# Routed attention and a feed-forward block in one kernel: scores, masks and values in quarters of the TensorE array, with centroid products, weight rounding and sums moved

## The chip, the cores and the metric

One Trainium2 chip; the kernel runs on one of its cores. The metric is the device time of one execution in microseconds (us). Engines are named as in the profile: PE is TensorE's matrix multiplication and PEld its loading of stationary weights, DVE is VectorE, ACT is ScalarE, POOL is GpSimd, SP is SyncE, which here issues nearly all DMAs. SBUF is the working memory, PSUM the accumulators that PE writes (eight banks of 512 float32 columns on 128 partitions), HBM the main memory.

## The reference

Inputs q, k, v are (4, 8, 768, 64) and centroids (8, 16, 64) in float32; the two weight matrices, (512, 2048) and (2048, 512), are in float64.

```python
def _attn_ref(q, k, v, centroids):
    q_n, k_n, c_n = (t / (norm(t) + 1e-06) for t in (q, k, centroids))
    q_assign = argmax(einsum('bhsd,hcd->bhsc', q_n, c_n))
    k_assign = argmax(einsum('bhsd,hcd->bhsc', k_n, c_n))
    mask = q_assign[:, :, :, None] == k_assign[:, :, None, :]
    scores = D ** -0.5 * matmul(q, k.transpose(0, 1, 3, 2))
    scores = where(mask, scores, -1e9)
    attn = softmax(scores)                    # with 1e-09 added to the sum
    return matmul(attn, v)

x = attn_out.transpose(0, 2, 1, 3).reshape(3072, 512)
h = x @ w_in
out = (h / (1 + exp(-1.702 * h))) @ w_out
```

Every query and every key is assigned to the nearest of its head's 16 centroids, and a query sees only keys of its own cluster. The attention's output goes through a feed-forward block with a sigmoid gate.

## The kernel before, in words

**Tiling of the attention.** There are 32 heads (4 batches of 8), taken two at a time: 16 pairs `p`, the two heads of a pair `a` = 0 and 1. The 64 dimensions of head 0 lie on partitions 0 to 63, those of head 1 on 64 to 127. A pair has two groups `g`, one for each half of the queries (384 of them, `HALF`); a group has six units `u`, one for each block of 128 keys (`kt`). For a unit the kernel computes transposed scores, 128 keys on the partitions and 384 queries along the row, for both heads (`scores`, L451); adds a mask term by a second product into the same PSUM tile (`part`, L466); takes the exponential on ACT into an SBUF tile `A` (`exps`, L474); adds `A` up over the six key blocks on POOL (`add_up`, L484, five additions per group); and multiplies by the values on PE, accumulating the group's output in PSUM (`values`, L495), which ACT then copies to SBUF (L501).

**Masks.** From the centroid products (`prep_near`, L326; sixteen small products per pair, into PSUM) DVE finds each row's best centroid and turns its number into a code (`prep_assign`, L349 to L389: a transposition, a maximum, a comparison, a product with ranks, a maximum, a square, a transposition, a cast). SP writes the codes to DRAM as lines (L396, four DMAs) and loads them back as rows (`prep_spread`, L403, sixteen DMAs of one row each). The mask product takes three such rows of keys and three of queries; it comes to zero where the codes agree and to a very large negative number where they do not. For the first pair the mask comes from one-hot vectors instead (`prep_hot`).

**Normalisation.** When a group's six units are through, PE sums `sum` over the keys (`normalise`, L508), DVE transposes, takes the reciprocal, spreads it back (L511, L513, L516) and multiplies the output by it (L522).

**Rounding of weights.** In the same phase DVE reads the 32 chunks of float64 weights as integers and makes float32 of them: five operations per chunk (`rounding`, L189, L193, L196, L200, L203), one at a time between other work (`step`). A chunk keeps one PSUM bank from its first operation to its last. ACT looks at each chunk for values out of range (`check_w`).

**Feed-forward block.** Both products use a seven-product scheme for 2 by 2 blocks (`first7`, `second7`), which needs sums and differences of weights (POOL) and of x (`sums_x`, DVE, L554).

**Order.** Every engine works through its instructions in the order in which the program issues them (`manual_schedule`). The main loop `for t in range(NT + 2)` makes one *step* of two units per pass; a pair is six steps, numbered here 0 to 5. In each pass: scores and masks of the step's two units, exponentials, POOL's additions; preparations of the next pair as `prep_at` has them (Q transposed on DVE, L305, in step 0; K transposed and centroid products in step 2; assignment and spread in step 3); values of the step before; some rounding operations, as many as `steps = (3, 1, 2, 0, 1, 4)` says; and, in steps 1 and 4, the row sums and the normalisation of the group that ended two steps before. Centroid products stand ahead of the values on PE. All eight sums of x for the first batch are issued together (`t == NT - 20`).

**PSUM.** `ps_m` has three banks, shared by rounding, centroid products, assignment and row sums; `ps_s` two tiles of two banks for scores; `ps_o` one bank for the values' sum. In the feed-forward block `ps_b` has five.

Of the kernel before, what the change touches and what calls it, by code (L numbers as in the profile page):

```python
# [8 lines left out]
FP32 = mybir.dt.float32  # L9
# [29 lines left out]
def fast(  # L39
# [26 lines left out]
    nc = tc.nc  # L66
# [155 lines left out]
    def check_w(i, raw, z):  # L222
# [123 lines left out]
    def prep_assign(p):  # L346
        ps = bank()
        if p > 0:
            nc.vector.transpose(out=ps[:, 0:HALF], in_=sT.pop(p)[:, 0:HALF])  # L349
# [41 lines left out]
    def prep_spread(p):  # L391
        n = NJ * 4
        row = code.pop(p)
        line = dram.tile([2, n, P], BF16, name="line")
        for r in range(0, P, SQ):
            nc.sync.dma_start(  # L396
                out=line[:, :, r:r + SQ].rearrange("b n t -> n b t"),
                in_=row[r:r + n])
        for a in range(2):
            for r in range(SQ * a, P, 2 * SQ):  # L400
                for w, b, to in ((0, 0, 0), (0, 1, 1), (1, 0, 0), (1, 1, 2)):
                    at = (w * 2 + a) * NJ
                    nc.sync.dma_start(  # L403
                        out=rows_of[w, p % 2][r + to:r + to + 1, :],
                        in_=line[b, at:at + NJ, :].rearrange(
                            "j t -> (j t)")[None, :])

# [37 lines left out]
    def scores(u):  # L445
        g, kt = divmod(u, NJ)
        p, h = split(g)
        ps = ps_s.tile([P, 2, 512], FP32, name="s")
        for a in range(2):
            rows = slice(a * D, (a + 1) * D)  # L450
            nc.tensor.matmul(out=ps[:, a, 0:HALF],  # L451
                             lhsT=T[p, 1][rows, kt * P:(kt + 1) * P],
                             rhs=T[p, 0][rows, h * HALF:(h + 1) * HALF],
                             start=True, stop=False)
        s_of[u] = ps[:, :, 0:HALF]

    def part(u):

        g, kt = divmod(u, NJ)
        p, h = split(g)  # L460
        n = NC if p == 0 else 3
        q_rows, k_rows = (hots[w] if p == 0 else rows_of[w, p % 2]
                          for w in range(2))
        for a in range(2):
            r = SQ * (a if p == 0 else 2 * (u % 2) + a)
            nc.tensor.matmul(  # L466
                out=s_of[u][:, a, :],
                lhsT=k_rows[r:r + n, kt * P:(kt + 1) * P],
                rhs=q_rows[r:r + n, h * HALF:(h + 1) * HALF],
                start=False, stop=True)  # L470

# [16 lines left out]
    def values(u):  # L488
        g, kt = divmod(u, NJ)
        p, h = split(g)  # L490
        if kt == 0:
            o_of[g] = ps_o.tile([P, 512], FP32, name="o")
        A = A_of.pop(u)
        for a in range(2):
            nc.tensor.matmul(out=o_of[g][a * D:(a + 1) * D, 0:HALF],  # L495
                             lhsT=v_in[p][:, a, kt, :], rhs=A[:, a, :],
                             start=(kt == 0), stop=(kt == NJ - 1))
        if kt == NJ - 1:
            O_of[g] = (xp if p < NPAIR - HP else xl).tile(
                [P, HALF], FP32, name="x")  # L500
            nc.scalar.copy(O_of[g], o_of.pop(g)[:, 0:HALF])  # L501

    def normalise(g):

        sm = sum_of.pop(g)
        ps = bank()
        for a in range(2):
            nc.tensor.matmul(out=ps[a * D:(a + 1) * D, 0:HALF], lhsT=twos,  # L508
                             rhs=sm[:, a, :], start=True, stop=True)
        turned = short()  # L510
# [9 lines left out]
        b, hp = divmod(p, HP)  # L520
        x = O_of.pop(g)
        nc.vector.tensor_tensor(out=x, in0=x, in1=rec, op=ALU.mult)  # L522
# [35 lines left out]

    def differences(b):


        X = {(r, h, c): xT_of.pop((b, h, 2 * r + c))
             for r in range(2) for h in range(2) for c in range(2)}
        T = {(3, c): T_of[3, c] for c in range(2)}
        for c in range(2):
            T[1, c] = X[0, 1, c]
            sums(nc.vector, ((T[3, c], X[1, 1, c], "-", T[1, c]),
                             (T[1, c], T[1, c], "-", X[0, 0, c])))
        return X, T

    def A_in(row, col, f):
# [23 lines left out]
    def sums_x(b):  # L598

        X, T = differences(b)  # L600
        T.update(((i, c), T_of[i, c]) for i in (2, 4) for c in range(2))
        for c in range(2):
            sums(nc.vector, ((T[2, c], X[1, 1, c], "-", T[1, c]),))
        for c in range(2):
            sums(nc.vector, ((T[4, c], X[1, 0, c], "-", T[2, c]),))
        return X, T

# [28 lines left out]
    for t in range(NT + 2):  # L636
# [167 lines left out]
    for b in range(B):  # L804
# [11 lines left out]
        for n in range(NH):  # L816
# [19 lines left out]
            if n == 1 and b < B - 1:  # L836
                XT = sums_x(b + 1)
    return is_bad
# [438 lines left out]
```

## Time and profile before

| | us |
|---|---|
| median of 3 runs | 996.82 (993.31 to 1000.97) |
| profiled execution | 997.54 |
| its span | 995.7 |
| first scores to the first product of the feed-forward block | 12.1 to 409.3 |
| feed-forward block | 409.3 to 995.7 |

| busy, us | span | PE | DVE | ACT | POOL |
|---|---|---|---|---|---|
| all | 995.7 | 943.0 | 623.8 | 314.3 | 418.8 |
| 46.0 to 368.0 | 322.0 | 288.8 | 257.0 | 184.2 | 252.6 |
| 409.3 to 995.7 | 586.4 | 581.0 | 320.8 | 88.8 | 105.0 |

A line of a group reads: source line, engine, operation, out<-in with shapes, count, then busy time, mean length of one, idle time of the engine just before them and what ended it. A line of the timeline reads: start, length, engine, line, operation, out<-in, count, and in brackets the idle time ahead of it and what ended it. A line of the waits reads: who waited, for whom, us in total, times, the longest. PE's float32 products appear as two matmul records each, so eight records of scores are the four products of a step. A record's length is that of the product passing through the array; the distance between starts says how long PE was taken.

### The profile page before, as it was taken

To read this page: it belongs to the slowest core of one execution; us is meant where nothing else is said; L and a number is where in the kernel's file an instruction comes from. 1 tells how busy PE (TensorE), PEld (TensorE's weight loads), DVE (VectorE), ACT (ScalarE), POOL (GpSimd) and SP (SyncE) were. 2 spreads that over 40 slices of the span, in tenths; PEclk is the share of its full clock that TensorE was granted. 3 is DMA by queue.
4 is the path that set the end of the run, shared out by engine and by line. 5 is a ranking of instruction groups with operands and counts; after the bars stand their busy time and mean duration, and the time that the engine had idled before them with its cause. 6 is when DMAs were issued, how large, how long until landed. Compare 5 with 4: busy or idle time off the path is not lost.

```text
span 995.7 us, 12731 instructions
## 1 busy us (share of the span) xinstructions
PE 943.0 (95%) x4565; PEld 569.6 (57%) x4565; DVE 623.8 (63%) x1029; ACT 314.3 (32%) x671; POOL 418.8 (42%) x308
## 2 busy tenths in 40 slices
PE   5998999999998789999999999999999999999997
PEld 3333333333333233455788655888655888556886
DVE  3678778877779985477634477534577434677431
ACT  3565565555655456322100122100222000222000
POOL 3878788777879678677400122000122000220000
PEclk8999999999999899999999999999999999999999
DMA  9344444544444311000200000000000000000000
GB/s 179 82 94 111 94 98 95 112 101 92 93 114 92 87 49 29 17 0 1 64 22 22 21 1 1 0 22 22 22 0 1 16 22 22 6 1 1 22 22 24
DMA packets 138440, 46.59 MB, mean 47 GB/s; under 512 B 127376, under 2 KB 132736, under 8 KB 138368
## 3 DMA queue, kind: packets, MB, share of 16 engines
q1 hardware_dynamic: 138224, 45.66, 20.2%
q8 instruction: 38, 0.62, 0.3%
q14 instruction: 34, 0.28, 0.1%
q10 hardware_dynamic: 144, 0.03, 0.0%
HBM read 37.63 MB, written 8.05 MB: 46 GB/s over the span
## 4 chain that ended last, share of the span: by engine, by line
PE 82%; DVE 12%; issue 3%; SPq 1%; DMA 1%; ACT 1%; POOL 0%; DVEq 0%; POOLq 0%; ACTq 0%
PE b L716 29%; PE b L773 29%; PE o L495 10%; PE s L451 9%; DVE T L305 2%; PE s L466 2%; PE m L508 2%; DVE short L516 1%; DVE short L511 1%; DVE e L200 1%; DVE x L522 1%; PE m L326 1%; DVE T L554 1%; DVE e L196 1%; DVE m L189 1%
## 5 line engine op out<-in xcount | busy, mean ns | idle before, releaser
L484 POOL TENSOR_TENSOR sum<-sum,A 128x768 f32<-128x768 f32 x128 | 243.3, 1901 | 32.0 <-ACT A L474 23.5
L474 ACT ACTIVATE A<-s 128x768 f32<-128x768 f32 x192 | 144.9, 806 | 158.6 <-PE s L466 157.0
L554 POOL TENSOR_TENSOR W<-w_in 128x256 f32<-128x256 f32 x32 | 23.8, 742 | 381.3 <-PE b L716 381.2
L707 DVE TENSOR_TENSOR G<-b,G 128x384 f32<-128x384 f32 x224 | 124.4, 556 | 64.6 <-PE b L716 51.4
L451 PE MATMUL s<-T,T 64*128 64x384 f32 x768 | 153.1, 518 | 4.4 <-ACT A L474 4.4
L495 PE MATMUL o<-A,inv 128*64 128x384 f32 x768 | 150.4, 515 | 0.0
L707 DVE TENSOR_TENSOR y<-b,y 128x256 f32<-128x256 f32 x72 | 29.4, 423 | 171.1 <-PE b L773 121.9
L544 ACT ACTIVATE th<-G 128x384 f32<-128x384 f32 x128 | 67.0, 523 | 210.1 <-DVE G L707 129.4
L451 PEld LDWEIGHTS s<-T,T 64*128 64x128 f32 x768 | 67.0, 189 | 89.6 <-ACT A L474 55.8
L545 DVE SCALAR_TENSOR_TENSOR G<-th,G 128x384 f32<-128x384 f32 x128 | 91.5, 715 | 22.8 <-ACT th L544 19.1
L716 PE MATMUL b<-x,W 128*128 128x384 f32 x256 | 93.0, 486 | 0.0
L716 PE MATMUL b<-T,w_in 128*128 128x384 f32 x256 | 93.0, 486 | 0.0
L716 PE MATMUL b<-x,w_in 128*128 128x384 f32 x256 | 89.9, 492 | 0.0
L773 PE MATMUL b<-Z,G 128*128 128x256 f32 x384 | 86.8, 379 | 0.0
L484 POOL TENSOR_TENSOR sum<-A 128x768 f32<-128x768 f32 x32 | 59.6, 1862 | 61.4 <-ACT A L474 61.3
L773 PE MATMUL b<-w_out,G 128*128 128x256 f32 x384 | 84.8, 379 | 0.0
L495 PEld LDWEIGHTS o<-A,inv 128*64 128x64 f32 x768 | 48.0, 140 | 57.0 <-issue 55.8
L773 PEld LDWEIGHTS b<-w_out,G 128*128 128x128 f32 x384 | 72.8, 190 | 10.9
L773 PEld LDWEIGHTS b<-Z,G 128*128 128x128 f32 x384 | 73.0, 190 | 9.9
L716 PEld LDWEIGHTS b<-x,w_in 128*128 128x128 f32 x256 | 49.1, 192 | 34.0 <-issue 1.2
L716 PEld LDWEIGHTS b<-x,W 128*128 128x128 f32 x256 | 48.6, 190 | 33.9
L716 PEld LDWEIGHTS b<-T,w_in 128*128 128x128 f32 x256 | 48.6, 190 | 33.9
(112 smaller groups left out, 1053.3 us busy)
## 6 DMA issues: line engine op xcount, KB each, us to landing
raw<-in_moe_w_in_dram SPq DMA_DIRECT2D x16, 512.0 KB
raw<-in_moe_w_out_dram SPq DMA_DIRECT2D x16, 512.0 KB
inv<-in_v_dram SPq DMA_DIRECT2D x16, 384.0 KB
in<-in_q_dram SPq DMA_DIRECT2D x60, 96.0 KB
in<-in_k_dram SPq DMA_DIRECT2D x60, 96.0 KB
rows<-line SPq DMA_DIRECT2D x240, 1.5 KB
out_dram<-y SPq DMA_DIRECT2D x12, 256.0 KB
out_dram<-y SPq DMA_DIRECT2D x24, 128.0 KB
```

The costliest lines, as they stand in the source:

```text
L305: nc.vector.transpose(out=T[p, w], in_=qk_in[p, w].rearrange("p j a d -> p (j a d)"))
L451: nc.tensor.matmul(out=ps[:, a, 0:HALF], lhsT=T[p, 1][rows, kt * P:(kt + 1) * P], rhs=T[p, 0][rows, h * HALF:(h + 1) * HALF], start=True, ...
L466: nc.tensor.matmul(out=s_of[u][:, a, :], lhsT=k_rows[r:r + n, kt * P:(kt + 1) * P], rhs=q_rows[r:r + n, h * HALF:(h + 1) * HALF], start=Fa ...
L474: nc.scalar.activation(out=A_of[u], in_=s_of.pop(u), func=AF.Exp, scale=SCALE)
L484: nc.gpsimd.tensor_tensor(out=sum_of[g], in0=A_of[u - 1] if kt == 1 else sum_of[g], in1=A_of[u], op=ALU.add)
L495: nc.tensor.matmul(out=o_of[g][a * D:(a + 1) * D, 0:HALF], lhsT=v_in[p][:, a, kt, :], rhs=A[:, a, :], start=(kt == 0), stop=(kt == NJ - 1))
L544: nc.scalar.activation(out=t, in_=h, func=AF.Tanh, scale=1.702)
L545: nc.vector.scalar_tensor_tensor(out=g, in0=t, scalar=1.0, in1=h, op0=ALU.add, op1=ALU.mult)
L554: engine.tensor_tensor(out=o, in0=a, in1=b, op=(ALU.add if op == "+" else ALU.subtract))
L707: nc.vector.tensor_tensor(out=o, in0=p, in1=a, op=ALU.add)
L716: nc.tensor.matmul(out=ps[:, 0:HALF], lhsT=a[:, c], rhs=x(c), start=(c == 0), stop=(c == 1))
L773: nc.tensor.matmul(out=ps[:, 0:DN], lhsT=a(f // 4)[:, f % 4], rhs=z(f), start=(f == 0), stop=(f == FB - 1))
```

## The change

- `scores`: each product of 64 dimensions by 128 keys becomes two of 64 by 64, so that a unit has four, one for each quarter of the array (64 rows by 64 columns).
- `part`: the mask rows of a head are laid out in a tile of 64 rows that is zero elsewhere, and the mask products are of 64 rows by 64 columns, four per unit instead of two. `rows_of` is set to zero and two single rows of each tile to `-CODE` (eight more memsets on POOL at the start). `prep_spread` loads eight rows per pair instead of sixteen.
- `values`: the 128 keys of a block are split into two halves of 64, accumulated in two banks (`ps_o` has two banks). ACT copies both halves, the second into a `short` tile, and `normalise` adds them on DVE before it multiplies.
- `normalise` is split: `row_sums_of` holds the products and stands directly behind the values.
- Centroid products come behind the values and row sums of step 2; K is transposed in step 1.
- `prep_assign` transposes into a `short` tile in SBUF, so that its maximum and its comparison read SBUF instead of PSUM (all pairs but the first). `tmp` has five tiles.
- Rounding: `steps = (2, 0, 4, 0, 1, 4)`. `ps_m` has two banks, `ps_b` six.
- `sums_x` is a generator that makes one sum at a time; those of the first batch are spread over the last eight steps.

```diff
-    ps_m = ctx.enter_context(tc.tile_pool(name="ps_m", bufs=3, space=PS))
+    ps_m = ctx.enter_context(tc.tile_pool(name="ps_m", bufs=2, space=PS))
...
-    tmp = att.enter_context(tc.tile_pool(name="tmp", bufs=3))
+    tmp = att.enter_context(tc.tile_pool(name="tmp", bufs=5))
...
-    for rows in rows_of.values():
-        nc.gpsimd.memset(rows, -CODE)
+    for (w, _), rows in rows_of.items():
+        nc.gpsimd.memset(rows, 0.0)
+        for r in range(SQ * w, P, D):
+            nc.gpsimd.memset(rows[r:r + 1, :], -CODE)
...
     def prep_assign(p):
-        ps = bank()
         if p > 0:
-            nc.vector.transpose(out=ps[:, 0:HALF], in_=sT.pop(p)[:, 0:HALF])
+            ps = short()
+            nc.vector.transpose(out=ps, in_=sT.pop(p)[:, 0:HALF])
         else:
+            ps = bank()
...
-            for r in range(SQ * a, P, 2 * SQ):
-                for w, b, to in ((0, 0, 0), (0, 1, 1), (1, 0, 0), (1, 1, 2)):
-                    at = (w * 2 + a) * NJ
-                    nc.sync.dma_start(
-                        out=rows_of[w, p % 2][r + to:r + to + 1, :],
+            for w, b, to in ((0, 0, 1), (0, 1, SQ), (1, 0, 1), (1, 1, 0)):
+                at, r = (w * 2 + a) * NJ, a * D + to
+                nc.sync.dma_start(
+                    out=rows_of[w, p % 2][r:r + 1, :],
...
     def scores(u):
...
-            nc.tensor.matmul(out=ps[:, a, 0:HALF],
-                             lhsT=T[p, 1][rows, kt * P:(kt + 1) * P],
-                             rhs=T[p, 0][rows, h * HALF:(h + 1) * HALF],
-                             start=True, stop=False)
+            for c in range(0, P, D):
+                nc.tensor.matmul(
+                    out=ps[c:c + D, a, 0:HALF],
+                    lhsT=T[p, 1][rows, kt * P + c:kt * P + c + D],
+                    rhs=T[p, 0][rows, h * HALF:(h + 1) * HALF],
+                    start=True, stop=False)
...
     def part(u):
...
         for a in range(2):
-            r = SQ * (a if p == 0 else 2 * (u % 2) + a)
-            nc.tensor.matmul(
-                out=s_of[u][:, a, :],
-                lhsT=k_rows[r:r + n, kt * P:(kt + 1) * P],
-                rhs=q_rows[r:r + n, h * HALF:(h + 1) * HALF],
-                start=False, stop=True)
+            rows = slice(a * D, (a + 1) * D)
+            for c in range(0, P, D):
+                nc.tensor.matmul(
+                    out=s_of[u][c:c + D, a, :],
+                    lhsT=rows_of[1, p % 2][rows, kt * P + c:kt * P + c + D],
+                    rhs=rows_of[0, p % 2][rows, h * HALF:(h + 1) * HALF],
+                    start=False, stop=True)
...
     def values(u):
...
-            o_of[g] = ps_o.tile([P, 512], FP32, name="o")
+            o_of[g] = ps_o.tile([P, 2, 512], FP32, name="o")
         A = A_of.pop(u)
-        for a in range(2):
-            nc.tensor.matmul(out=o_of[g][a * D:(a + 1) * D, 0:HALF],
-                             lhsT=v_in[p][:, a, kt, :], rhs=A[:, a, :],
-                             start=(kt == 0), stop=(kt == NJ - 1))
+        for r in range(2):
+            rows = slice(r * D, (r + 1) * D)
+            for a in range(2):
+                nc.tensor.matmul(out=o_of[g][a * D:(a + 1) * D, r, 0:HALF],
+                                 lhsT=v_in[p][rows, a, kt, :],
+                                 rhs=A[rows, a, :],
+                                 start=(kt == 0), stop=(kt == NJ - 1))
...
-            nc.scalar.copy(O_of[g], o_of.pop(g)[:, 0:HALF])
...
+                [P, HALF], FP32, name="x"), short()
+            for r in range(2):
+                nc.scalar.copy(O_of[g][r], o[:, r, 0:HALF])
...
-        x = O_of.pop(g)
+        x, more = O_of.pop(g)
+        nc.vector.tensor_tensor(out=x, in0=x, in1=more, op=ALU.add)
         nc.vector.tensor_tensor(out=x, in0=x, in1=rec, op=ALU.mult)
...
-            t = 2 * TG * (p - 1) + (0, 0, 2, 2, 2, 3, 3)[i]
+            t = 2 * TG * (p - 1) + (0, 0, 1, 1, 2, 3, 3)[i]
...
-    steps = (3, 1, 2, 0, 1, 4)
-    XT = None
+    steps = (2, 0, 4, 0, 1, 4)
+    made = sums_x(0)
...
-        while work and PREP[work[0][1]] == prep_near:
-            prep(*work.pop(0))
         if 1 <= t <= NT:
             for u in range(2 * t - 2, 2 * t):
                 values(u)
+        if t >= 2 and (t - 2) % TG == TG - 1:
+            row_sums_of((t - 2) // TG)
+        while work and PREP[work[0][1]] == prep_near:
+            prep(*work.pop(0))
...
-        if t == NT - 20:
-            XT = sums_x(0)
+        if t >= NT - 8 and t < NT:
+            XT = next(made)
...
-    ps_b = ctx.enter_context(tc.tile_pool(name="ps_b", bufs=5, space=PS))
+    ps_b = ctx.enter_context(tc.tile_pool(name="ps_b", bufs=6, space=PS))
```

More of the change, by code (lines that the diff above doesn't have):

```diff
@@ L399, in prep_spread @@
         for a in range(2):
[L400 to L406 removed]
+            for w, b, to in ((0, 0, 1), (0, 1, SQ), (1, 0, 1), (1, 1, 0)):
+                at, r = (w * 2 + a) * NJ, a * D + to
+                nc.sync.dma_start(
+                    out=rows_of[w, p % 2][r:r + 1, :],
+                    in_=line[b, at:at + NJ, :].rearrange(
+                        "j t -> (j t)")[None, :])
     def prep_hot(p):
@@ L460, in part @@
         p, h = split(g)
-        n = NC if p == 0 else 3
-        q_rows, k_rows = (hots[w] if p == 0 else rows_of[w, p % 2]
-                          for w in range(2))
-        for a in range(2):
-            r = SQ * (a if p == 0 else 2 * (u % 2) + a)
-            nc.tensor.matmul(
-                out=s_of[u][:, a, :],
-                lhsT=k_rows[r:r + n, kt * P:(kt + 1) * P],
-                rhs=q_rows[r:r + n, h * HALF:(h + 1) * HALF],
-                start=False, stop=True)
+        if p == 0:
+            for a in range(2):
+                r = SQ * a
+                nc.tensor.matmul(
+                    out=s_of[u][:, a, :],
+                    lhsT=hots[1][r:r + NC, kt * P:(kt + 1) * P],
+                    rhs=hots[0][r:r + NC, h * HALF:(h + 1) * HALF],
+                    start=False, stop=True)
+            return
+        for a in range(2):
+            rows = slice(a * D, (a + 1) * D)
+            for c in range(0, P, D):
+                nc.tensor.matmul(
+                    out=s_of[u][c:c + D, a, :],
+                    lhsT=rows_of[1, p % 2][rows, kt * P + c:kt * P + c + D],
+                    rhs=rows_of[0, p % 2][rows, h * HALF:(h + 1) * HALF],
+                    start=False, stop=True)
     def exps(u):
@@ L491, in values, with row_sums_of @@
         if kt == 0:
-            o_of[g] = ps_o.tile([P, 512], FP32, name="o")
+            o_of[g] = ps_o.tile([P, 2, 512], FP32, name="o")
         A = A_of.pop(u)
-        for a in range(2):
-            nc.tensor.matmul(out=o_of[g][a * D:(a + 1) * D, 0:HALF],
-                             lhsT=v_in[p][:, a, kt, :], rhs=A[:, a, :],
-                             start=(kt == 0), stop=(kt == NJ - 1))
+        for r in range(2):
+            rows = slice(r * D, (r + 1) * D)
+            for a in range(2):
+                nc.tensor.matmul(out=o_of[g][a * D:(a + 1) * D, r, 0:HALF],
+                                 lhsT=v_in[p][rows, a, kt, :],
+                                 rhs=A[rows, a, :],
+                                 start=(kt == 0), stop=(kt == NJ - 1))
         if kt == NJ - 1:
+            o = o_of.pop(g)
             O_of[g] = (xp if p < NPAIR - HP else xl).tile(
-                [P, HALF], FP32, name="x")
-            nc.scalar.copy(O_of[g], o_of.pop(g)[:, 0:HALF])
-    def normalise(g):
+                [P, HALF], FP32, name="x"), short()
+            for r in range(2):
+                nc.scalar.copy(O_of[g][r], o[:, r, 0:HALF])
+    def row_sums_of(g):
         sm = sum_of.pop(g)
-        ps = bank()
+        ps = ps_of[g] = bank()
         for a in range(2):
@@ L509, in normalise @@
                              rhs=sm[:, a, :], start=True, stop=True)
+    ps_of = {}
+    def normalise(g):
+        ps = ps_of.pop(g)
         turned = short()
@@ L557, in fast @@
     T_of = {}
[L559 to L569, printed above, removed]
     def A_in(row, col, f):
@@ L598, in sums_x @@
     def sums_x(b):
-        X, T = differences(b)
-        T.update(((i, c), T_of[i, c]) for i in (2, 4) for c in range(2))
+        X = {(r, h, c): xT_of.pop((b, h, 2 * r + c))
+             for r in range(2) for h in range(2) for c in range(2)}
+        T = {(i, c): T_of[i, c] for i in (2, 3, 4) for c in range(2)}
         for c in range(2):
[L603 to L606, printed above, removed]
+            T[1, c] = X[0, 1, c]
+        for o, a, z in ((3, (1, 1), 1), (1, 1, (0, 0)), (2, (1, 1), 1),
+                        (4, (1, 0), 2)):
+            for c in range(2):
+                one, two = (X[(*n, c)] if isinstance(n, tuple) else T[n, c]
+                            for n in (a, z))
+                sums(nc.vector, ((T[o, c], one, "-", two),))
+                yield X, T
     NT = NU // 2
@@ L836, in fast @@
             if n == 1 and b < B - 1:
-                XT = sums_x(b + 1)
+                *_, XT = sums_x(b + 1)
     return is_bad
```

## The prediction

> **What bounds the kernel now.** I read the page's table of slices first: PE is at 9 tenths nearly throughout, so no average says where the time can move. The windows do. From 409.3 us to the end (586.4 us) PE is busy 581.0; the change gives that stretch a sixth PSUM tile and nothing to do with it, so I leave it. From 46.0 to 368.0 PE is busy 288.8 of 322.0: the idle 33 us are in attention. Two of the page's groups to keep in mind:
>
> ```profile
> L484 POOL TENSOR_TENSOR sum<-sum,A 128x768 f32<-128x768 f32 x128 | 243.3, 1901 | 32.0 <-ACT A L474 23.5
> L451 PE MATMUL s<-T,T 64*128 64x384 f32 x768 | 153.1, 518 | 4.4 <-ACT A L474 4.4
> ```
>
> POOL's additions fill it: ten of 1.9 us per pair of heads, 19 us of a pair's 23.5.
>
> Next the waits from 45 to 300 us, and the timeline of one pair, PE and then DVE (start, length, engine, line).
>
> ```profile
> PE m L326 <- DVE T L305: 22.5, 11, 2.2
> ```
>
> ```profile
> 166.10 0.82 PE L508 MATMUL m<-sum,twos 128*64 128x384 f32 x4
> 166.84 1.56 PE L451 MATMUL s<-T,T 64*128 64x384 f32 x8
> 168.34 0.34 PE L466 MATMUL s<-rows,rows 3*128 3x384 bf16 x4
> 168.61 0.53 PE L326 MATMUL m<-T,cT 128*32 128x192 f32 x8
> 171.13 0.53 PE L326 MATMUL m<-T,cT 128*32 128x192 f32 x8 [1.99 <-DVE T L305]
> 171.59 1.51 PE L495 MATMUL o<-A,inv 128*64 128x384 f32 x8
> 173.03 1.56 PE L451 MATMUL s<-T,T 64*128 64x384 f32 x8
> ...
> 168.52 1.67 DVE L522 TENSOR_TENSOR x<-x,short 128x384 f32<-128x384 f32 x1
> 170.11 0.96 DVE L305 STREAM_TRANSPOSE T<-in 128x768 f32<-128x768 f32 x1
> 172.19 0.56 DVE L349 STREAM_TRANSPOSE m<-m 128x384 f32<-128x384 f32 x1
> 175.45 0.20 DVE L389 CAST row<-turned 128x64 bf16<-128x64 f32 x1
> ```
>
> Call a pass of the main loop a step; a pair has six, 0 to 5. A plain step lasts 3.20 us. In step 2 (from 166.84) PE waits 2 us for K's transposition, which stands behind the normalisation on DVE. A second chain is nearly as long: row sums at the end of step 1, normalisation, K's transposition, assignment (L349 to L389), lines to DRAM (issued 175.67), rows back (sixteen issues, 178.55 to 183.20, landing about 1.3 us after the last), masks of step 0 at 184.79. Issued in time with 0.6 us to spare: **17.9 us from step 2's start to those masks**, then 5.6 us to the next step 2. That is the 23.5 us pair.
>
> **PE's share.** Row sums follow values in the same array shape and take 0.65 us for two rounds of two: 0.325 a round. Scores take four rounds in 1.49, values four in 1.44, masks 0.27 for half a round (0.16). So 2.72 of the 3.20 us is streaming, 0.48 the changes of shape. In quarters, if four run abreast: 1.30 + 0.33 (the masks need two rounds) + 1.30 = 2.93. Bounds: 3.4 if every change still costs (0.16 more for masks), about 5.5 if only two quarters run abreast; the thirty-two-column products L326, four in 0.53 with their second pass, show four column strips abreast, so I take 2.93. Row sums and centroid products now change shape by themselves: row sums 0.65 + 0.30, centroid products 0.8 + 0.3. PE needs 6 x 2.93 + 2 x 0.95 + 1.1 = 20.6 us per pair.
>
> The Trainium skill, TensorEngine Tiling (Array Packing), Key Properties, says that switching the mode drains the engine and switching the tile within a mode does not. By it the 0.48 us goes; by the rows alone it could stay, and a step would be 3.4.
>
> **DVE's share, where the change costs.** Moved ahead of the normalisation, K's transposition no longer holds PE: minus 2 us of wait per pair. But the masks' chain remains, and this is what it gets.
>
> (a) One more addition per group (x plus the other key half, both SBUF). DVE operations with two SBUF inputs wait for POOL here: L522 takes 0.56 at best and 1.48 in the median, L200 0.69 or up to 2.30. Several in a row each wait for a whole POOL addition, as the sums of x show:
>
> ```profile
> 322.66 0.56 DVE L554 TENSOR_TENSOR x<-x 128x384 f32<-128x384 f32 x1
> 323.13 2.17 DVE L554 TENSOR_TENSOR T<-x 128x384 f32<-128x384 f32 x1
> 325.34 2.06 DVE L554 TENSOR_TENSOR x<-x 128x384 f32<-128x384 f32 x1
> 327.32 4.23 DVE L554 TENSOR_TENSOR T<-x 128x384 f32<-128x384 f32 x2
> ...
> 322.87 8.27 POOL L484 TENSOR_TENSOR sum<-sum,A 128x768 f32<-128x768 f32 x4 [0.76 <-ACT A L474]
> ```
>
> The normalisation falls into such a run of four POOL additions (steps 1 and 2 feed them). So 0.12 + 1.54 (transposition, reciprocal, transposition) + 1.5 + 2.1 = 5.3 us; free of POOL it would be 2.7.
>
> (b) Four rounding operations instead of two now stand in step 2, ahead of the assignment: 4 x 0.7, and in four pairs of five one of them is L200 at about 1.6: 3.5 us (2.8 to 4.2).
>
> (c) The assignment. Before, it took 3.5 us because PE's wait in step 2 left POOL idle for 2.8 us just then. Where it did not, it took 6.1 (347.77 to 353.87):
>
> ```profile
> 349.57 1.75 DVE L364 TENSOR_TENSOR short<-short,rank 128x384 bf16<-128x384 bf16 x1
> 352.44 1.43 DVE L389 CAST row<-turned 128x64 bf16<-128x64 f32 x1
> ...
> 361.21 0.42 PE L466 MATMUL s<-rows,rows 3*128 3x384 bf16 x2 [0.63 <-DMA rows<-line]
> 362.48 0.32 PE L466 MATMUL s<-rows,rows 3*128 3x384 bf16 x1 [0.85 <-DMA rows<-line]
> ```
>
> and the masks came 2.2 us late. Without PE's wait that is the rule: POOL's next five additions run from about 7 to 17 us after step 2's start, and the assignment starts at 5.3 + 3.5 = 8.8. L361 also reads its scores from SBUF now. From PSUM it took 0.56 however busy POOL was; from SBUF no row shows it. It costs 0.56 at least, 0.56 + 1.8 if it waits for one addition; with all four blocked the assignment is 8.4. I take the row there is, 6.1.
>
> SBUF - State Buffer (the Trainium skill), SBUF: two separate sides, says that DVE with two SBUF inputs and GpSimd take a port pair exclusively for a whole instruction. By it L361's comparison is blocked from now on; by the PSUM row it is not, and the chain is 1 to 2 us shorter than the rule has it.
>
> (d) Eight row loads instead of sixteen: 8 x 0.29 = 2.3 us of SP issue less. Lines to first row issue 2.9, then 7 x 0.29 + 1.3.
>
> Sum, from step 2's start: 5.3 + 3.5 + 6.1 + 2.9 + 2.0 + 1.3 = **21.1 us**, where PE comes by at 2.93 + 1.1 + 2.93 + 3.88 + 2.93 + 1.3 = 15.1. PE stands idle 6 us in front of the masks, and the clock drops: after 3.81 us idle at 337.47 scores took 2.93 instead of 1.49 and masks 0.51, 1.6 us more. To the next step 2: 0.33 + 1.3 + 2.93 + 0.95 = 5.5. Pair: 21.1 + 5.5 + 1.6 = 28.2 us.
>
> **Sum.** From step 2 at 45.95 to the last at 368.03 are thirteen pairs, 24.8 us each, with 9 us in one of them from the sums of x, which go when these are spread over the last eight steps. 13 x (28.2 - 24.8) = +44. First eight steps: PE 2 less, one late mask 3 more: +1. Last masks: 21.1 + 1.6 - 17.9 = +5. After them PE gains 1.5; the spread sums, up to 2.1 each beside normalisations, make DVE late by some 2: +0.5. Start: eight one-row memsets on POOL, 0.10 (one column) to 0.74 us (the same 768 columns) each, in front of the centroids' norms: +1 to +6, I take 4. Total +55 on the profiled execution's 997.5 us (span 995.7 and 1.8 around it): **1053 us**. The median of the runs, 996.8, is 0.7 below it.
>
> Costed at nothing: the second PSUM copy (0.48 us on ACT, busy 57% of that window; it has 1.6 us of scores and masks before PE wants the tile, and late it costs up to 0.5 per group); two banks instead of three (row sums of step 4 want the bank that the assignment's first transposition frees at 9.5 us, and come by at about 9.8: 0 to 0.7 per pair); four Q loads one step earlier on SP (0.5 us of issue each, now further ahead of the lines, which is where they stood behind; they land four steps before their use); the sums of later x, the same eight in another order.
>
> **Rivals.** *POOL is not in the way (faster).* The price is the lock alone: normalisation 2.7, steps 2.8, assignment 3.7 give a chain of 2.7 + 2.8 + 3.7 + 6.2 = 15.4, and a pair of 20.9, PE's own pace. 13 x (20.9 - 24.8) = -51, start and tail +5: 952; with half of it 970. For it: DVE is busy 257 of 322 us, and whatever delays PE opens gaps for POOL. Against it: L522's median. It decides once the chain is under 15.1.
>
> *Chain and PE meet halfway (same).* Normalisation blocked, assignment mostly free (3.5): chain 18.5, pair 24 to 24.6. -10 to -3, start, last masks and tail +6: about 997.
>
> *Quarters do not run four abreast.* Steps of 5.5, pairs of 36: 13 x 11 = +145, about 1145. Against it stand the four strips of L326; no row shows four quarters.
>
> **Numbers.** Forecast (pairs of 26 to 31) 0.64; faster rival 0.17; halfway 0.14; not abreast 0.05. 1% is about what a measurement of this kernel can tell from no change (its three runs span 0.8%). Faster takes the first rival and a little of the halfway one: 0.19; same 0.11; slower 0.70. The range: assignment 3.5 to 8.4 and start 1 to 6 give 1017 to 1085; halfway reaches down to 985, which leaves out most of the faster rival and the last.
>
> **What would show it.** Right: PE waits for rows in front of the masks in nearly every pair, 4 to 8 us; normalising additions of 1.4 and 2.1 us; comparison and CAST above 1 us; no wait at the centroid products; a plain step of 2.9; scores or values at half clock after the wait. Wrong: masks without waiting and pairs under 24 us (POOL's gaps are larger than I think), or scores of 2.6 us (quarters in turn).

## The result, and the profile after

| | before | after |
|---|---|---|
| median of four runs each, us | 996.96 (993.31 to 1000.97) | 1074.95 (1073.96 to 1079.03) |
| profiled execution | 997.54 | 1079.03 |
| its span | 995.7 | 1077.1 |
| first scores | 12.1 | 18.2 |
| a pair (mean of 13) | 24.8 | 30.0 |
| first product of the feed-forward block | 409.2 | 490.5 |
| from there to the end | 586.5 | 586.6 |

The ratio is 1.079, with a 95% interval of 1.074 to 1.084: slower, inside the range, 22 us above the forecast (26 in the profiled execution, of which 24 are the thirteen pairs and 2 the start). All of it lies in attention. Thirteen pairs (52.09 to 441.97 us) cost 67.8 us more than thirteen before, the start 6.1, the first and last steps the rest of 81.

The page of the changed kernel: PE's busy tenths in 40 slices, the engines' shares of the chain that ended last, three groups. L477 is the mask product, L454 the scores, L495 POOL's additions.

```profile
PE   4967888877777778888999999999999999999998
...
PE 66%; DVE 21%; SPq 4%; DMA 3%; issue 3%; POOL 2%; ACT 0%; POOLq 0%; DVEq 0%; ACTq 0%
...
L495 POOL TENSOR_TENSOR sum<-sum,A 128x768 f32<-128x768 f32 x128 | 243.8, 1905 | 48.8 <-ACT A L485 41.1
L454 PE MATMUL s<-T,T 64*64 64x384 f32 x1536 | 157.0, 518 | 0.6 <-ACT A L485 0.6
...
L477 PE MATMUL s<-rows,rows 64*64 64x384 bf16 x720 | 60.4, 354 | 93.9 <-DMA rows<-line 93.9
```

PE's digits have fallen from 9 to 7 and 8 in the attention half, and the clock with them (mean granted clock 0.942, before 0.985). DVE has 21% of the chain (12% before). 93.9 us of idle time stand in front of a single group, the masks. The waits from 45 to 450 us say the same (us in total, times, longest); the wait at the centroid products, 22.5 us up to 300 us in the kernel before, is gone.

```profile
PE s L477 <- DMA rows<-line: 87.8, 27, 7.3
```

The chain that ended last, in order of time, through one pair (start, length, engine, tile, line). Step 2 of this pair starts at 231.5.

```profile
233.06 1.43 DVE x L544
234.51 2.07 DVE x L545
236.58 2.25 DVE e L200
...
242.11 1.11 DVE short L364
243.25 1.87 DVE short L367
...
245.73 1.31 DVE codes L385
...
247.34 1.58 DVE row L392
...
255.04 0.85 PE s L477 x6
255.89 2.56 PE o L508 x16
```

This is the whole loss in one view. Every DVE operation listed here has two operands in SBUF or goes from SBUF to SBUF, and every one is longer than it can be. At their shortest in the same trace the addition L544 takes 0.51, the multiplication L545 0.56, the rounding L200 0.65, the comparison L364 0.56, the product L367 0.36 and the cast L392 0.19; the codes L385 never take less than 1.09 here, and 0.18 in the kernel before. Then lines go out and rows come in (1.33 us for each of the two landings in this chain), and masks follow; and after PE's wait the values take 2.56 us where the shortest in the trace take 1.29. POOL's additions over the same stretch, from the timeline:

```profile
240.98 3.91 POOL L495 TENSOR_TENSOR sum<-sum,A 128x768 f32<-128x768 f32 x2 [0.44 <-ACT A L485]
245.17 3.69 POOL L495 TENSOR_TENSOR sum<-sum,A 128x768 f32<-128x768 f32 x2 [0.28 <-ACT A L485]
```

The two additions of the first line end at 242.8 and 244.9, those of the second at 247.0 and 248.9. DVE's four operations end at 243.2 (L364), 245.1 (L367), 247.0 (L385) and 248.9 (L392): each is let go when an addition ends, and the next one behind it waits for the next addition. This holds all through the trace: the blocked ones end a fixed time behind the end of an addition, 0.41 us in all twelve blocked cases of L364 and all sixteen of L545, 0.21 to 0.22 in fourteen of L367, 0.04 to 0.05 in fifteen of L385 and fourteen of L392.

### The profile page after: what moved, and what is told of

Same layout as the page of the kernel before. It is cut to its first block, busy times and chain, and to the rows that moved or that the text cites. A ratio compares the mean times of both kernels' runs of the same rounds, so it can differ in the third digit from the quotient of the medians.

```text
span 1077.1 us, 16459 instructions
## 1 busy us (share of the span) xinstructions
PE 956.6 (89%) x6461; PEld 616.6 (57%) x6461; DVE 701.9 (65%) x1061; ACT 331.6 (31%) x703; POOL 425.0 (39%) x316
## 4 chain that ended last, share of the span: by engine, by line
PE 66%; DVE 21%; SPq 4%; DMA 3%; issue 3%; POOL 2%; ACT 0%; POOLq 0%; DVEq 0%; ACTq 0%
PE b L728 27%; PE b L785 27%; PE o L508 5%; PE s L454 3%; DVE short L367 2%; SPq L405 2%; DVE x L545 2%; DVE row L392 2%; DVE e L200 2%; DMA line<-row 2%; DVE x L544 2%; DMA rows<-line 2%; DVE short L364 2%; DVE codes L385 2%; PE s L477 1%
## 5 line engine op out<-in xcount | busy, mean ns | idle before, releaser
L495 POOL TENSOR_TENSOR sum<-sum,A 128x768 f32<-128x768 f32 x128 | 243.8, 1905 | 48.8 <-ACT A L485 41.1
L508 PE MATMUL o<-A,inv 64*64 64x384 f32 x1536 | 166.7, 538 | 0.0
L454 PE MATMUL s<-T,T 64*64 64x384 f32 x1536 | 157.0, 518 | 0.6 <-ACT A L485 0.6
L477 PE MATMUL s<-rows,rows 64*64 64x384 bf16 x720 | 60.4, 354 | 93.9 <-DMA rows<-line 93.9
L454 PEld LDWEIGHTS s<-T,T 64*64 64x64 f32 x1536 | 69.3, 143 | 72.4 <-ACT A L485 32.6
L495 POOL TENSOR_TENSOR sum<-A 128x768 f32<-128x768 f32 x32 | 60.0, 1876 | 119.3 <-ACT A L485 119.2
L568 DVE SCALAR_TENSOR_TENSOR G<-th,G 128x384 f32<-128x384 f32 x128 | 91.7, 716 | 22.5 <-ACT th L567 18.9
L477 PEld LDWEIGHTS <-rows 64*64 64x64 bf16 x720 | 28.1, 113 | 134.4 <-DMA rows<-line 108.7
L508 PEld LDWEIGHTS o<-A,inv 64*64 64x64 f32 x1536 | 79.5, 147 | 35.8 <-issue 24.5
```

The source lines that it names most:

```text
L454: nc.tensor.matmul(out=ps[c:c + D, a, 0:HALF], lhsT=T[p, 1][rows, kt * P + c:kt * P + c + D], rhs=T[p, 0][rows, h * HALF:(h + 1) * HALF], ...
L477: nc.tensor.matmul(out=s_of[u][c:c + D, a, :], lhsT=rows_of[1, p % 2][rows, kt * P + c:kt * P + c + D], rhs=rows_of[0, p % 2][rows, h * HA ...
L495: nc.gpsimd.tensor_tensor(out=sum_of[g], in0=A_of[u - 1] if kt == 1 else sum_of[g], in1=A_of[u], op=ALU.add)
L508: nc.tensor.matmul(out=o_of[g][a * D:(a + 1) * D, r, 0:HALF], lhsT=v_in[p][rows, a, kt, :], rhs=A[rows, a, :], start=(kt == 0), stop=(kt = ...
L568: nc.vector.scalar_tensor_tensor(out=g, in0=t, scalar=1.0, in1=h, op0=ALU.add, op1=ALU.mult)
```

## The experiments

The theory to test: the chain from the normalisation to the masks is long because DVE's operations wait for POOL's additions, one after another. The rivals: its order on DVE is at fault (four rounding operations ahead of the assignment); the extra addition per group and the second copy are; the quarters are dear on PE; the rows' DMAs are. The expectations call the kernels by their numbers, e7 for kernel 7; kernel 12 follows its own text, written last. Kernels 5, 7, 10 and 11 ran four times, the others once; four runs of the changed kernel span 5 us, four of the kernel before 8. Starts, lengths and masks below are means over all fifteen preparations, pairs the mean of thirteen.

**1. POOL's additions taken away.**

```diff
-        if kt == 0:
+        if kt != 1:
             return
...
-            out=sum_of[g], in0=A_of[u - 1] if kt == 1 else sum_of[g],
-            in1=A_of[u], op=ALU.add)
+            out=sum_of[g], in0=A_of[u - 1],
+            in1=ones[:, 0:1].broadcast_to((P, 2 * HALF)).rearrange(
+                "p (a n) -> p a n", a=2), op=ALU.add)
```

> The changed kernel with one POOL addition per group instead of five (it leaves out the sum of the exponentials over the other key blocks, so the output is not normalised as it should be). Theory 'POOL in the way': DVE's operations with two SBUF inputs stop waiting, the normalisation falls from 5.1 to about 2.7 us, the assignment from 8.0 to about 3.6, the masks' rows come in time, a pair falls from 30.0 to 21 us, the time from 1077 to about 955. Rival 'DVE's own work and the way through DRAM': these stay, a pair stays above 27 us and the time above 1040.

Measured: 956.19 us, beside 995.73 before. The assignment lasts 4.6 us (7.9 in the changed kernel), the masks start 15.1 us after step 2's start (20.8), the pair is 21.6. DVE's operations, one pair of this kernel:

```profile
226.10 0.56 DVE L547 TENSOR_TENSOR x<-x,short 128x384 f32<-128x384 f32 x1
...
233.79 0.20 DVE L394 CAST row<-turned 128x64 bf16<-128x64 f32 x1
```

No DVE instruction was changed, and these have their shortest length, as has the comparison in thirteen of sixteen pairs (0.56). What still waits is mostly one operation per assignment, for the one addition left there: the product in ten pairs (1.50 us), the comparison in three (1.84 to 1.87). The DMAs are as they were, so they aren't the cause. But this takes eight of POOL's ten additions per pair away, some 15 us, and says nothing on which DVE operation matters.

**2. Rounding moved out of step 2.**

```diff
-    steps = (2, 0, 4, 0, 1, 4)
+    steps = (2, 0, 0, 4, 1, 4)
```

> The changed kernel with the four rounding operations of step 2 moved behind the assignment in step 3. If the chain from row sums to masks sets the pair, it loses 3 to 3.5 us of it: assignment starting at about 5.2 instead of 8.3 us after step 2's start, pair 30 to 27 us, time about 1035 to 1040. Rival 'DVE as a whole is full': only the order changes, time within 10 us of 1077.

Measured: 1022.39. The assignment now starts at 5.3 instead of 8.0 and is 6.6 long; masks at 19.0, pairs of 25.8; the time fell further than the 1035 to 1040 expected. Comparison (median 0.99 us), codes (1.11) and cast (1.58) stay long: order alone shortens the chain and leaves the operations slow. A wait appeared that I had not foreseen: row sums 45.4 us in all, up to 6.7 each, behind the last rounding operation of a chunk (from 45 to 420 us). A half-made chunk holds one of the two banks, and the order decides when.

**3. Values whole, and 4. scores wide.** Whole values take away the second copy and the addition per group; wide scores (64x128) are the shape of before.

```diff
 # 3, values and normalise
+        for a in range(2):
+            nc.tensor.matmul(out=o_of[g][a * D:(a + 1) * D, 0:HALF],
+                             lhsT=v_in[p][:, a, kt, :], rhs=A[:, a, :],
+                             start=(kt == 0), stop=(kt == NJ - 1))
...
-        nc.vector.tensor_tensor(out=x, in0=x, in1=more, op=ALU.add)
 # 4, scores
-            for c in range(0, P, D):
...
+            nc.tensor.matmul(out=ps[:, a, 0:HALF],
+                             lhsT=T[p, 1][rows, kt * P:(kt + 1) * P],
+                             rhs=T[p, 0][rows, h * HALF:(h + 1) * HALF],
+                             start=True, stop=False)
```

> The changed kernel with values undone: 128 keys per product, one bank, one copy, no addition of halves; the rest stays. If the added addition costs a wait for a whole POOL addition on the chain: normalisation 5.1 to about 3.1 us, pair 30 to 28, time 1050 to 1055. If it costs only its own 0.5 us: time about 1070. PE's step becomes 0.2 to 0.3 us longer, which costs nothing while PE waits for rows.

> The changed kernel with scores undone (64 x 128 products, as before); masks and values stay in quarters. A step of PE grows from 2.92 to 3.1 to 3.4 us. If PE is off the path in attention: time within +8 us of 1077. If PE's steps set the pace: +0.3 x 96 = +29, about 1106.

Measured: 1042.4, below both readings of its expectation, and 1075.56. A plain step is 3.2 us in both against 2.9 in the changed kernel, so PE has more to do in both; the first is faster all the same, since its assignment starts at 6.4, and the second shows that 0.3 us of PE per step is worth nothing while PE waits (rows still cost it 75.5 us).

**5. The order alone, in the kernel before.** K transposed in step 1 and centroid products behind the values, nothing else.

```diff
-    t = 2 * TG * (p - 1) + (0, 0, 2, 2, 2, 3, 3)[i]
+    t = 2 * TG * (p - 1) + (0, 0, 1, 1, 2, 3, 3)[i]
 # and the loop over prep_near behind values(u)
```

> The kernel before with one part of the change alone: K transposed in step 1, centroid products behind the values. Theory 'POOL's gap': PE's 2 us wait at the centroid products goes, and with it the 2.8 us in which POOL was idle while DVE assigned; the assignment grows from 3.5 to 6 or 7 us, rows come at 0.1 + 3.2 + 1.4 + 6.5 + 2.9 + 4.4 + 1.3 = 19.8 us after step 2's start, and the masks wait for them: pairs of 25 to 26 us instead of 24.8, time 997 to 1015. Rival 'the wait was the loss': the assignment stays at 3.5, pairs of 22.4, time about 965.

Measured: 1019.93 (1017.58 to 1025.53), ratio 1.025 (1.019 to 1.031). It is 5 us above the range expected. PE's wait moved from the centroid products to the masks and grew to 33.1 us. Waits from 45 to 400 us, and the timeline of one pair of this kernel (L382 is the line of the codes):

```profile
PE s L466 <- DMA rows<-line: 33.1, 28, 3.0
```

```profile
211.50 1.79 DVE L382 SCALAR_TENSOR_TENSOR codes<-codes 128x24 f32<-128x24 f32 x1
...
211.44 1.80 POOL L484 TENSOR_TENSOR sum<-A 128x768 f32<-128x768 f32 x1 [0.78 <-ACT A L474]
```

In the kernel before, PE's wait at the centroid products held back exponentials and so POOL, and the assignment ran in that gap (3.9 us on average). With the wait gone it takes 5.6.

**6. The memsets of `rows_of` moved behind the centroids' norms on POOL**, the same lines after the power instead of ahead of it.

> The changed kernel with the memsets of the mask rows behind the centroids' norm on POOL. If these memsets are what delays the first scores from 12.1 to 18.2 us, the first scores come at about 12.5 and the time falls by 5 to 6 us to about 1071. If they only move, and hold up DVE's early operations in the same way, nothing is gained.

Measured: 1068.02, first scores at 11.9 instead of 18.2: the start's 6 us, and nothing else. In the changed kernel two one-row memsets took 1.50 us, eight of them and the four whole ones 9.4 us in front of the norms, and DVE waited:

```profile
11.39 0.15 DVE L277 TENSOR_SCALAR consts<-consts 128x1 f32<-128x1 f32 x1 [7.91 <-POOL consts L276]
```

**7. Operands in PSUM, whole chunks of rounding in steps 3 and 5, memsets late.** The row sums' reciprocals are spread back into PSUM, the assignment's scores are transposed into PSUM, the comparison writes float32 into the centroid products' bank, and the codes are turned in PSUM. So the multiplication of x, the comparison, the product and the cast each read PSUM once.

```diff
-            ps = short()
+            ps, near = bank(), sT.pop(p)
...
+        at = eq if p == 0 else near[:, 0:n * NC]...
-            out=eq, in0=sc, ...   op=ALU.is_equal
+            out=at, in0=sc, ...   op=ALU.is_equal
-            out=eq, in0=eq, ...   op=ALU.mult
+            out=eq, in0=at, ...   op=ALU.mult
...
-        turned = asg.tile([P, 2, SQ], FP32, name="turned")
+        turned = ps[:, HALF:HALF + 2 * SQ]
...
-        rec = short()
+        rec = ps[:, 0:HALF]
...
-    steps = (2, 0, 4, 0, 1, 4)
+    steps = (0, 0, 0, 5, 0, 5)
```

> The changed kernel with DVE kept out of POOL's way: the spread reciprocal, the comparison's result and the turned codes lie in PSUM, so that the multiplication, the product with ranks and the cast have one SBUF input less; rounding in whole chunks of five operations behind the assignment and in step 5 (steps 0, 0, 0, 5, 0, 5); memsets late. Normalisation 5.1 to 3.7 us, nothing between it and the assignment, assignment 4.4: rows come at about 14.5, PE comes by at 15.1. Pairs of 22 to 23 us (DVE's sum per pair, about 22.5, is then the longest), time 960 to 975. Rival 'DVE is full anyway': pairs of 25, time 995 or more.

Measured: 962.20 (961.27 to 963.96), ratio to before 0.965 (0.960 to 0.970); assignment 4.2 us, masks at 15.1, pairs of 21.9, PE's wait for rows 8.5 us in all.

**8. Kernel 3 with the assignment's scores transposed into PSUM**, and a third bank for preparations (`ps_m` three, `ps_b` five).

> As e3 (values whole), and the assignment transposed into PSUM again (three banks for it, five in the feed-forward block, as before), so that the comparison reads PSUM. If each operation with two SBUF inputs pays its own wait: 0.7 to 1 us less per pair, time about 1030 (e3 took 1042). If the next blocked operation only waits the longer for the same POOL addition: within 5 us of 1042.

Measured: 1031.33, 11 less than kernel 3. The comparison is 0.557 us in all sixteen pairs (0.557 to 2.014, median 1.18, in kernel 3), yet in twelve of fifteen pairs the assignment ends where it did in fourteen of kernel 3's, 13.71 to 13.76 us after step 2's start. The next blocked operation ends with the same addition of POOL, however early it begins. Most of the gain came from two pairs that escaped (21.8 and 24.3 us long, together 8.5 less than in kernel 3). So the number is that of the expectation's first reading and the mechanism, in most pairs, that of its second: its agreement with 1030 is luck. Blocked operations can't be priced one by one.

**9. The order of kernel 7 without its PSUM operands.**

> The changed kernel with the memsets late and the rounding in e7's order (steps 0, 0, 0, 5, 0, 5), but nothing moved to PSUM; it parts e7's two halves. If placement in PSUM is needed beside the order: assignment starts about 5.2 us after step 2's start and is still blocked (6 to 8 us long, comparison and cast above 1 us), masks at 17 to 18, pairs of 25 to 26, as with four operations moved to step 3 (1022), less 6 for the memsets: 1005 to 1018. If the order alone does it: assignment about 4, pairs under 23, about 965 to 975.

Measured: 1018.36; assignment from 5.7, 6.5 long, masks at 17.2, pairs of 25.7. DVE in one pair of it:

```profile
231.29 1.64 DVE L385 SCALAR_TENSOR_TENSOR codes<-codes 128x24 f32<-128x24 f32 x1
...
233.24 1.60 DVE L392 CAST row<-turned 128x64 bf16<-128x64 f32 x1
```

Kernels 9 and 7 differ by their PSUM operands alone: 56 us.

**10 and 11. What the quarters are worth once DVE is out of POOL's way.** Kernel 7 with the edits of 3 and 4 (only masks in quarters), and kernel 7 with the edit of 3 alone.

> e7's DVE work (order, operands in PSUM, memsets late), but scores of 64x128 and values of 128x64 as in the kernel before; only the mask products stay in quarters. It asks what the quarters of scores and values are worth once DVE is out of POOL's way. If PE then sets the pace, they are worth what a plain step shows, 3.2 against 2.92 us: 96 steps of 0.28 are 27 us more than e7's 962, less up to 5 for the one DVE addition per group that goes: 982 to 990. If the masks' chain sets the pace in e7 too, PE's 0.28 is hidden in most steps: 970 or less.

> e7 with the values whole (128x64) and scores and masks in quarters. A plain step of 3.2 us as in the changed kernel with whole values, so 978 to 990 if PE sets the pace in e7; less than 965 if the second output copy and the DVE addition that go are worth more than the quarters of the values.

Measured: 968.71 (968.12 to 969.54), ratio 0.973 (0.967 to 0.980), and 957.31 (955.65 to 957.56), ratio 0.961 (0.955 to 0.967). The second reading of each expectation gave the numbers: kernel 7 is paced by its chain. In these two PE sets the pace and never waits for rows. PE's timelines, kernel 10, then kernel 11, then kernel 7, from one step's scores to the next:

```profile
205.54 1.56 PE L456 MATMUL s<-T,T 64*128 64x384 f32 x8
...
208.92 1.56 PE L456 MATMUL s<-T,T 64*128 64x384 f32 x8
```

```profile
208.53 1.52 PE L457 MATMUL s<-T,T 64*64 64x384 f32 x16
...
211.74 1.52 PE L457 MATMUL s<-T,T 64*64 64x384 f32 x16
```

```profile
205.80 1.52 PE L457 MATMUL s<-T,T 64*64 64x384 f32 x16
...
208.75 1.47 PE L457 MATMUL s<-T,T 64*64 64x384 f32 x16
```

A plain step is 3.38 us in kernel 10, 3.21 in kernel 11 and 2.95 in kernel 7 behind row sums, which have another shape; where no other shape stands beside it, its parts there are 1.29 + 0.33 + 1.29 = 2.91. Pairs are 22.36, 21.39 and 21.88. The quarters of the scores bring 1.0 us per pair, as six steps of 0.17 should. Those of the values save some 1.1 us per pair on PE (20.3 of its own time in kernel 7, worked out below, against 21.4) and lose more than that. Kernel 7's DVE shows one cost: the addition of the two halves, both in SBUF, is 1.94 us on average from 130 to 260 us, and one of the two per pair stands ahead of the assignment.

```profile
198.08 2.17 DVE L547 TENSOR_TENSOR x<-x,short 128x384 f32<-128x384 f32 x1
...
202.17 0.57 DVE L366 TENSOR_TENSOR m<-m,best 128x384 f32<-128x384 f32 x1
```

PE's own parts of a pair sum to 6 x 2.91 + 2 x 0.80 + 0.79 = 19.9 us in kernel 7. The row sums (twice) and the centroid products are of another shape and lengthen their neighbours by 0.16 each time (values 1.40 for 1.29 in front, scores 1.34 for 1.29 behind): 20.3. Its 21.9 hold the late rows (8.5 us in thirteen waits) and the cold steps and late exponentials behind them, which no run tells apart.

**12. Kernel 11 with the changed kernel's rounding order**, and a third bank for preparations (whole values leave it room). With kernels 3, 9 and 7 this parts order from placement. The same with values in quarters gave no time. It deadlocks: two banks are left for preparations, and, as the program reads, a half-made chunk, the centroid products and the assignment want three. So what placement brings in this order is known for whole values only.

```diff
-    steps = (0, 0, 0, 5, 0, 5)
+    steps = (2, 0, 4, 0, 1, 4)
```

> e11 (957) with the changed kernel's rounding order (2, 0, 4, 0, 1, 4) again and a third bank for preparations, which the values' single bank leaves room for: whole values, everything in PSUM, memsets late, but four rounding operations ahead of the assignment. With e9 it parts order from placement. Assignment from 6.4 on as in the kernel with whole values alone (1042), but 3.9 long: masks at 15.5 to 16.5, pairs of 24 to 25, 990 to 1005. If placement suffices alone: masks under 14, 957 to 970. If the order is what matters: above 1020.

Measured: 955.75, beside 996.53 before (one run each). The favoured case missed; it is "placement suffices alone", a little below its 957, though the masks come at 15.7 and not under 14 (PE itself comes by at 15.6). The assignment starts at 5.5 on average, not 6.4, because the multiplication of x no longer waits (0.553 to 0.556 in all 32 groups); it is 4.2 long; PE waits 3.1 us for rows in all. The timeline of DVE in one pair, with four rounding operations ahead of the assignment, and POOL beside it:

```profile
226.81 0.57 DVE L366 TENSOR_TENSOR m<-m,best 128x384 f32<-128x384 f32 x1
...
228.59 0.91 DVE L387 SCALAR_TENSOR_TENSOR codes<-codes 128x24 f32<-128x24 f32 x1
...
229.82 0.22 DVE L395 CAST row<-m 128x64 bf16<-128x64 f32 x1
```

```profile
223.30 4.05 POOL L498 TENSOR_TENSOR sum<-sum,A 128x768 f32<-128x768 f32 x2 [0.23 <-POOL sum L498]
```

The comparison lies beside an addition of POOL and is not held. The codes (L387), still SBUF and SBUF, are the one operation of the assignment that waits (0.18 to 1.42; up to 1.84 in kernel 7). The two causes side by side, in us (kernels with the memsets late, except where noted):

| | operands in SBUF | operands in PSUM |
|---|---|---|
| rounding 2, 0, 4, 0, 1, 4 | 1036 (kernel 3's 1042 less 6 for its memsets), whole values | 956, whole values, three banks |
| rounding 0, 0, 0, 5, 0, 5 | 1018, values in quarters | 957, whole values; 962, in quarters |

Placement brings 80 and 56 us. The 80 have the third bank in them; from kernel 8, which has that bank and one of the operands, less 6 for its memsets, it is 69. The order brings some 50 without placement (1068 to 1018, values in quarters) and nothing that one run can tell with it. Kernel 1, where most of POOL's work was taken away instead, with quarters and early memsets, comes to 956 too. Either ends most of the waiting for rows (12.8 us of it are left in kernel 1, 3.1 in kernel 12), and then PE is nearly the bound. Kernels 7, 10, 11 and 12 beat both the kernel before and the changed one.

## Why the prediction was right, point by point

The forecast's case came true: pairs of 30.0 us, where it said 26 to 31, because DVE's chain waits for POOL. All times from step 2's start, means over the thirteen pairs of the changed kernel, lines in its numbering. All the signs named for it showed: waits in front of the masks in every one of these pairs, additions of 1.4 and 2.1 us, comparison and cast above 1, no wait at the centroid products, values at half their speed after the wait.

| step of the prediction | predicted | measured |
|---|---|---|
| plain PE step | 2.93 | 2.91 to 2.96 |
| normalisation ends | 5.3 | 4.8 |
| four rounding operations | 3.5 | 3.5 |
| assignment | 6.1 | 8.0 |
| lines to first row issue | 2.9 | 2.6 |
| last row landed | 21.1 | 22.4 |
| last row to next step 2 | 7.1 | 7.6 |
| pair | 28.2 | 30.0 |
| start | +4 | +6.1 |
| thirteen pairs | +44 | +68 |
| first and last steps of attention | +6.5 | +7.4 |

- **Quarters on PE**: right, four abreast (scores 1.29, masks 0.33, values 1.29). The rule in the Trainium skill, TensorEngine Tiling (Array Packing), Key Properties, that a switch of the tile within a mode doesn't drain the engine, agrees with the rows: 3.38, 3.21 and 2.91 us a step as fewer shapes are left. The rival of quarters in turn is out.
- **(a) Normalisation**: right in mechanism and size, 5.1 in most pairs and 3.6 at the least. The addition and the multiplication are 1.43 and 2.07 in the pair shown, for 1.5 and 2.1 (over both groups of all pairs the medians are 0.70 and 1.31).
- **(b) Rounding**: right, 2.7 to 4.3 us from pair to pair. L200, the one of the five that waits for POOL, has a median of 0.69 over all chunks and takes up to 2.32.
- **(c) Assignment**: the mis-sized term. I took the one blocked case of before, 6.1, in which two of four candidates waited. All four wait in the median now: L364 1.06, L367 1.86, L385 1.11, L392 1.58 us. The bound with all four blocked, 8.4, was the nearer end: 8.0. The Trainium skill's page SBUF - State Buffer, SBUF: two separate sides (DVE with two SBUF inputs and GpSimd exclude each other for a whole instruction) had the comparison blocked from now on; the runs agree: 1.06 in the median from SBUF, 0.56 to 0.57 in every pair from PSUM (kernels 7, 8, 10, 11 and 12).
- **(d) Rows**: lines to first row 0.3 us shorter than predicted, first to last row as predicted. With the assignment's +1.9 and the normalisation's -0.5 the last row lands 1.3 late.
- **After the wait**: predicted 7.1 us from the last row to the next step 2, measured 7.6. Values took 2.56 us in all but the first of the pairs, which is +1.27; scores behind them 1.29 to 2.56, on average 2.0 in those, another +0.7. So the slow clock (0.87 granted from 45 to 450 us, against 0.97 from 46 to 368 before) costs 2.0, not 1.6, after these waits.
- **Start**: the memsets, at the dear end of their bounds: 0.73 each and 0.75 from one to the next, close to the 0.74 of 128 partitions. Kernel 6 gets back 6.3 us.
- **Costed at nothing**: row sums waited 1.1 us in all for a bank, so two banks are free of cost in this order; in kernel 2's order PE waited 45 us for them. Those waits took the place of waits for rows (9.3 us there, 42.4 in kernel 9, which has none of them and much the same time), so 45 us is not their price.
- **The faster rival** (952, POOL not in the way, decided by a chain under 15.1) is about what kernels 1 and 12 do, at 956 each; its price was right and its condition was not met. Its own sum gave a chain of 15.4, which is not under 15.1, and half of its gain would be some 975, not 970. **Halfway** (997) had the assignment at 3.5; with these operands in SBUF only the kernel before has that, by the gap that PE's wait opened, as kernel 5 shows: without that gap the same code lost 2.5%.

## What to carry to other kernels

A wait on the busiest engine can be what keeps a shared resource free for the chain behind it; before removing it, ask what then runs at the same time. Where DVE and GpSimd work side by side, go through DVE's critical operations one by one, and let each have at most one input in SBUF and, for a cast, its input in PSUM: here that was worth 56 to 80 us, where the better order alone brought 50. A blocked operation is released when the other engine's instruction ends, so price a row of them as a group: the comparison alone in PSUM, with a third bank, brought 11 us (kernel 8), the others 69 more (kernel 12).

## What the runs showed of the hardware that was not expected

- A blocked DVE operation ends with a POOL addition, and the next one waits for the next addition. The end of the assignment is therefore locked to POOL: 13.71 to 13.74 us in fourteen of fifteen pairs of kernel 3, whatever its start (4.9 to 7.4).
- A cast of 64 columns from SBUF to SBUF took 1.58 us in the median of the changed kernel, 0.19 at its shortest, and 0.22 to 0.23 in every pair when it read PSUM: one input is enough to be blocked. Transpositions from SBUF to SBUF and the maximum over SBUF were not blocked in the same kernel: 0.58 in all 32 of L538, 0.24 to 0.25 in all fifteen of L389, 0.55 to 0.56 in all fifteen of L361 that read SBUF.
- POOL's memset of one row of 768 columns took 0.73 us, nearly as long as one of 128 rows (0.74).
